# A two-layer decode step on one core: five load transfers merged at the two ends of its stream, and the last group's outgoing product made narrow

## The chip, the core and the metric

The kernel runs on one core of a Trainium2 chip. The metric is device time in microseconds, the median of the runs shown. Inside the core five engines work side by side: TensorE (PE in the profile, its weight loads PEld), VectorE (DVE), ScalarE (ACT), GpSimd (POOL) and SyncE (SP). All large loads are issued by SP and carried by 16 DMA engines into one big on-chip array, `arena`.

## The reference

One token goes through attention, MLP, attention, MLP. Both attention layers use the same weights and the same cache, and so do both MLPs. 32 heads, 4096 cached positions, head size 128, model width 512, MLP width 1376.

```
def _A_ref(x, k_cache, v_cache, wq, wo):
    q = (x @ wq).reshape(B, Sq, H, Dh)          # 1 token
    scores = einsum("bhqd,bhkd->bhqk", q, k_cache) * (Dh ** -0.5)
    o = einsum("bhqk,bhkd->bhqd", softmax(scores), v_cache)
    return o.reshape(B, Sq, H * Dh) @ wo
def _B_ref(x, w1, b1, w2, b2):
    return einsum("bsf,fd->bsd", gelu(x @ w1 + b1), w2) + b2
x = x + _A_ref(_layernorm(x), ...);  x = x + _B_ref(_layernorm(x), ...)
x = x + _A_ref(_layernorm(x), ...);  x = x + _B_ref(_layernorm(x), ...)
```

K and V are 64 MiB each. They don't fit on the chip, so almost all of both is read twice, in 32-bit floats.

## The kernel before, in words

The 32 heads are 8 groups of 4. A group's K is 8 blocks (`C = 8`) of 128 x 2048, 1 MiB each, and so is its V. Three regions of `arena` (A_AT, B_AT, C_AT) hold K and V in turn, so that SP can issue a load as soon as the region's former contents have been read. `load` (line 106) issues one transfer on SP; `blocks` (line 351) cuts a K or V into pieces and yields its blocks, and whoever uses a block waits for the whole piece that it came in.

For each group `group` (line 399) multiplies the queries with the 8 K blocks (`scores`: four 8 x 512 products per block), takes the softmax (`exponentials`, `weights`: a chain of small steps on DVE, one activation on ACT, four transposes on PE), and `values` multiplies the weights with V blocks (four 4 x 512 products per block). In most groups PE does two or three V blocks and DVE the others (`weighted`, `added`), and their sum and the outgoing product with wo of group n ride inside the scores of group n+1: behind block 4 comes `sum_up` with `head`, and `out_product` comes behind block 6, in the last group behind block 7.

The last group of each layer is different: PE does all 8 V blocks, V comes in the pieces of `LAST` (line 54), K in two halves, and two dummy products `idle(pS)` (128 x 512, no result) stand behind V blocks 5 and 7. Then comes `head_out` with a narrow outgoing product (16 products of 1 x 128 instead of 4 of 128 x 512), and the MLP (`mlp`): four w1 steps, the gelu on DVE and ACT, and 11 w2 blocks of four 1 x 128 products each, followed by the sum and the store of the result.

At the change of layers the loads share little room: `load_w1(SHARED, 3, 4)` may be issued only when `head` has read its scratch (line 290), the pieces of w2 (`W2_AT_CHANGE`) only when a w1 step has been read, and the next layer's weights and K (`behind_w2`) behind w2 blocks 3, 7 and 9. At the end, w1 and w2 (`W1_AT_END`, `W2_AT_END`, lines 53 and 56) go to free room and are issued early.

Each engine runs its instructions in the order in which the code emits them where `keep_in_program_order` is used: all loads on SP, all products on PE. What a block waits for is set by which piece it is in; what SP waits for is set by region reuse and by a ring of eight completion semaphores, each of which must be free before it is used again.

Small values live in two tiles, `cells` and `front`; `small` (line 83) puts them in the gaps of `cells`. The maximum `m` of the softmax lies in such a gap, inside the 128 columns that the wide outgoing product reads as its weights, so that in the last group line 233 waits for that product.

Of the kernel before, what the change touches and what calls it, by code (L numbers as in the profile page):

```python
# [23 lines left out]
C = 8  # L24
# [21 lines left out]
HALVES = ((0, 4), (4, 8))  # L46
# [4 lines left out]
FRONT = 192  # L51
CELLS = 239
W1_AT_END = ((0, 2), (2, 3), (3, 4))
LAST = ((0, 4), (4, 6), (6, 7), (7, 8))
W2_AT_CHANGE = ((0, 2), (2, 5), (5, 8), (8, 10), (10, 11))
W2_AT_END = ((0, 4), (4, 8), (8, 10), (10, 11))


@with_exitstack
def decode_layers(ctx: ExitStack, tc: tile.TileContext, vectors, k, v, w, w1, w2, out):  # L60
# [13 lines left out]
    ident, zq, wide = front[:, :P], front[:, P : P + ZQ], cells[:, :WIDE]  # L74
# [8 lines left out]
    def small(name, n=1):  # L83
        nonlocal first_front, rest
        if name.startswith("gelu_"):
            i = "huaztg".index(name[-1])
            return cells[:, gelu + FB * i : gelu + FB * (i + 1)]
        if name not in places:
            fit = [j for j in range(J) if gaps[j] + n <= ends[j]]
            if name == "by_dma":  # L90
                places[name] = front, first_front, n
                first_front += n
            elif fit:
                places[name] = cells, gaps[fit[0]], n
                gaps[fit[0]] += n
            else:
                places[name] = cells, rest, n
                rest += n
        t, a, m = places[name]
        assert m == n and first_front <= FRONT and rest <= CELLS  # L100
        return t[:, a : a + n]

    def at(first, n):
        return arena[:, first : first + n]

    def load(first, src):
        t = at(first, src.shape[-1])
        tc.keep_in_program_order(nc.sync.dma_start(t, src))  # L108
        return t

    def matmul(*a, **kw):
        tc.keep_in_program_order(nc.tensor.matmul(*a, **kw))  # L112
# [4 lines left out]
    def part(src, g, a, b):  # L117
        return src[g][:, NC * a : NC * b]
# [11 lines left out]
    by_dma = small("by_dma", FB + 8)  # L130
# [13 lines left out]
    pS, pO = (psum.tile([P, 512], F32, name=n) for n in ("pS", "pO"))  # L144
# [10 lines left out]
    def of_32(t, n, i=0):  # L155
        return t[:, : 32 * n].rearrange("p (c q) -> p c q", q=32)[:, :, i]

    def in_quarters(t, n):
        return t[:, : 32 * J].rearrange("p (j n) -> p j n", j=J)[:, :, :n]
# [4 lines left out]
    def turned(src, wide=False, to=None):  # L164

        t = turned_at[0] if to is None else to
        if wide:
            for j in range(J):
                q = slice(32 * j, 32 * j + 32)
                turn = nc.vector.transpose(t[q], src[q, P * j : P * (j + 1)])  # L170
                if src is pS:
                    tc.keep_in_program_order(turn)
        else:
            nc.vector.transpose(t, src[:, :P])  # L174
        return t
# [108 lines left out]
    def head(rl, last=False):  # L284
        ot = at(SCRATCH, U)
        nc.vector.transpose(ot, pO)  # L286
        o, on = small("o", 4), on_wide
        own = at(SCRATCH, 4 * 129).rearrange("p (b q) -> p b q", q=129)[:, :, :P]
        own = own.rearrange("p b (d q) -> p d b q", q=32)[:, :, :, 0]
        nc.vector.tensor_reduce(o, own, axis=AX.X, op=ALU.add)  # L290
        if last:
            nc.vector.tensor_scalar(on[:, :4], o, rl, None, op0=ALU.mult)  # L292
        else:
            nc.vector.tensor_scalar(in_quarters(on, 4), o.unsqueeze(1).to_broadcast([P, J, 4]), rl, None,
                                    op0=ALU.mult)
        return on
# [7 lines left out]
    def out_product(on, wt, to, narrow=False):  # L304
        for d in range(4):
            if narrow:
                for j in range(J):
                    matmul(to[32 * j : 32 * j + 1, :P], on[:, d : d + 1], wt[:, d, P * j : P * (j + 1)],
                           start=(d == 0), stop=(d == 3))
            else:  # L310
                matmul(to, on[:, d : d + P], wt[:, d, :], start=(d == 0), stop=(d == 3))
# [47 lines left out]
    def blocks(src, g, home, pieces=((0, C),)):  # L359
        for a, b in pieces:  # L360
            load(home + NC * a, part(src, g, a, b))
            for c in range(a, b):
                yield c, quarters(home + NC * c)
# [29 lines left out]
    def add_up(acc, own):  # L393
        t = small("acc", 4)
        nc.vector.scalar_tensor_tensor(t, own, 1.0, acc, op0=ALU.mult, op1=ALU.add)
        return t


    def group(z, acc, ahead, k_blocks, out_behind=C - 2):
        for c, t in k_blocks:  # L400
            scores(z, c, t)
            if ahead and c == SUM_BEHIND:
                t, rl, wt = ahead
                sum_up(t)
                on = head(rl)
            if ahead and c == out_behind:
                out_product(on, wt, pO)
        p = exponentials(sc, nsc)
        if ahead:
            acc = add_up(acc, of_32(turned(pO, wide=True), 4))  # L410
        return acc, *weights(p)

    def partly(pt, v_blocks, home, by_pe=BY_PE):
# [6 lines left out]
    negm, z, sc, nsc = first_queries(xs, s, wq_t, wide=True)  # L420
    acc = pairs(xs)[:, :, 0]
    ahead = None
    for g in range(G):
        final = g == G - 1
        k_home, v_home = RING[2 * g % 3], RING[(2 * g + 1) % 3]
        acc, pt, rl = group(z, acc, ahead, blocks(k, g, k_home, HALVES if final else ((0, C),)))
        ahead = None
        if g == G - 2:
            nc.scalar.copy(at(KEPT_K, 2 * U), at(k_home + NC * C - 2 * U, 2 * U))
        if g < G - 2:  # L430
            partly(pt, blocks(v, g, v_home), v_home)
            pair = load(PAIR, of_w(g % 2, g, 2))
            z = next_queries(xs, negm, by_four(pair[:, NC:]), to=pS)
            ahead = added(v_home), rl, by_four(pair[:, :NC])
            continue
        for c, t in blocks(v, g, v_home, LAST if final else ((0, C),)):
            values(c, pt, t, c)
            if final and c in (5, 7):
                idle(pS)
            if g == G - 2:  # L440
                for j in range(J):
                    i = 4 * c + j - KEPT_V // U
                    if i >= 0:
                        nc.scalar.copy(pK[i], t[j])
        if final:
            wo_t = by_four(load(PAIR, of_w(g % 2, g, 1)))
            for i in range(3):
                load_w1(SHARED, i, i + 1)
            own = head_out(rl, wo_t, last=True, home=ident)
            load_w1(SHARED, 3, 4)  # L450
        else:
            pair = load(PAIR, of_w(g % 2, g, 2))
            acc = add_up(acc, head_out(rl, by_four(pair[:, :NC])))
            wq_t = by_four(pair[:, NC:])
            z = next_queries(xs, negm, wq_t)
# [25 lines left out]
    g = G - 2  # L481
    negm, z, sc, nsc = first_queries(xs, s, wq_t)
    make_identity(nc, ident)
    acc = pairs(xs)[:, :, 0]
# [14 lines left out]
    pt, rl = weights(p)  # L499
# [3 lines left out]
    acc = add_up(acc, of_32(turned(pO), 4))  # L503

    v_t = [at(B_AT + U * i, U) for i in range(KEPT_V // U)]
    for i, first in enumerate([SHARED, SHARED + U] + [PAIR + U * j for j in range(4)]):
        t = at(first, U)
# [4 lines left out]
    pt, rl = weights(exponentials(sc, nsc))  # L512
    for c in range(C):
        values(c, pt, v_t[4 * c : 4 * c + 4], c)
    acc = add_up(acc, head_out(rl, by_four(pair[:, NC:])))
    z = next_queries(xs, negm, by_four(pair[:, :NC]))

    turned_at[0] = at(TURNED, P)
    homes, ahead = (A_AT, C_AT, B_AT), None
    for n in range(2, G):  # L520
        g, final = G - 1 - n, n == G - 1
        k_home, v_home = homes[(2 * n - 1) % 3], homes[2 * n % 3]
        acc, pt, rl = group(z, acc, ahead, blocks(k, g, k_home, HALVES if final else ((0, C),)),
                            C - 1 if final else C - 2)
        if not final:
            by_pe = BY_PE_AT_BEGIN if n == 2 else BY_PE
            partly(pt, blocks(v, g, v_home, ((0, 6), (6, 8)) if n == 2 else ((0, C),)), v_home, by_pe)
            pair = load(PAIR, of_w(g % 2, g - 1, 2))
            z = next_queries(xs, negm, by_four(pair[:, :NC]), to=pS)
            ahead = added(v_home, by_pe), rl, by_four(pair[:, NC:])  # L530
            continue
        for c, t in blocks(v, g, v_home, LAST):
            values(c, pt, t, c)
            if c in (5, 7):
                idle(pS)
        wo_t = by_four(load(PAIR, of_w(g % 2, g, 1)))
        for a, b in W1_AT_END:
            load_w1(A_AT, a, b)
        for a, b in W2_AT_END:
            load_w2(A_AT + 11 * U, a, b)  # L540
        own = head_out(rl, wo_t, last=True)
# [46 lines left out]
```

## Time and profile before

| | us |
|---|---|
| device time, three runs | 673.83, 673.91, 1145.31 |
| median | 673.91 |
| profiled execution, first to last instruction (its span) | 670.3 |
| DMA queue of SP, share of 16 engines | 99.1% |
| PE busy | 384.4 |
| DVE busy | 372.6 |
| loaded from memory | 285.6 MB |

Of the profiled execution the page gives the span and not the time around it; the two undisturbed runs are 3.5 and 3.6 us above the span. One run of 1145.31 lies far from the others; the median is not moved by it.

In the rows, a line number is that of the kernel printed above; all products issued through the helper have line 112 and all loads line 108, so they are told apart by their shapes. A row of a timeline gives start, duration, engine, line, operation, output and input, the count of merged instructions, and in brackets the idle time before it and what ended it. One product of the code is two matrix instructions in the trace. PEclk is the granted TensorE clock, 1.00 for full speed. Shares of DMA in short stretches can pass 1.00, since a packet's bytes and time are spread over it.

### The profile page before, as it was taken

What the parts mean: (1) busy time and instruction counts of PE and PEld (TensorE: products, weight loads), DVE (VectorE), ACT (ScalarE), POOL (GpSimd) and SP (SyncE); (2) the same over time, 40 slices, a digit from 0 to 9 for tenths busy, and PEclk for the clock granted to TensorE, in tenths of its full rate; (3) what the DMA queues carried; (4) which work ended last, traced back from release to release, by engine and by line L of the source; (5) the groups of instructions that cost most, each with busy time, mean ns of one, the idle gap of its engine ahead of it and who ended that gap; (6) DMA issues with size and microseconds to landing.
All of it is one profiled execution on the core that took longest, in us unless ns stands there. A gap on an engine that the chain in (4) does not pass through costs nothing. (4 is left out here: it accounts for less than half of the span.)

```text
span 670.3 us, 5537 instructions
## 1 busy us (share of the span) xinstructions
PE 384.4 (57%) x2342; PEld 109.2 (16%) x2342; DVE 372.6 (56%) x480; ACT 22.8 (3%) x48; POOL 4.8 (1%) x23
## 2 busy tenths in 40 slices
PE   3533842636618546286768878737617456074586
PEld 1101210101102101021214222111102112011122
DVE  2059388395793965932112221392893966938822
ACT  0010000000000000002000110000000000000000
POOL 1000000000000000000000000000000000000000
PEclk9567785877678658778979998977669868687789
DMA  9999999999999999999999999999999999999996
GB/s 376 438 439 438 434 438 438 405 464 435 438 430 408 430 438 439 438 438 421 426 416 402 431 452 423 437 440 431 426 434 416 457 439 438 435 423 407 438 420 286
DMA packets 11256, 285.97 MB, mean 427 GB/s; under 512 B 1504, under 2 KB 1504, under 8 KB 3296
## 3 DMA queue, kind: packets, MB, share of 16 engines
q1 hardware_dynamic: 11088, 285.61, 99.1%
q8 instruction: 18, 0.29, 0.2%
q14 instruction: 6, 0.05, 0.0%
q10 hardware_dynamic: 144, 0.01, 0.0%
HBM read 285.62 MB, written 0.00 MB: 426 GB/s over the span
## 5 line engine op out<-in xcount | busy, mean ns | idle before, releaser
L264 DVE TENSOR_TENSOR arena<-arena 128x2048 f32<-128x2048 f32 (+4 forms) x44 | 260.7, 5924 | 16.6 <-DMA arena<-in_v 15.9
L112 PE MATMUL pS<-arena,front 128*8 128x512 f32 x1036 | 152.0, 713 | 174.9 <-DMA arena<-in_k 164.5
L112 PE MATMUL pO<-arena 128*4 128x512 f32 x504 | 81.7, 800 | 26.1 <-DMA arena<-in_v 24.5
L112 PE MATMUL pO<-arena,cells 128*128 128x512 f32 (+4 forms) x376 | 82.7, 506 | 17.2 <-POOL cells L186 6.7
L112 PEld LDWEIGHTS pS<-arena,front 128*8 128x8 f32 x1036 | 30.6, 102 | 289.1 <-DVE arena L264 141.9
L286 DVE STREAM_TRANSPOSE arena<-pO 128x512 f32<-128x512 f32 x16 | 11.5, 717 | 110.1 <-PE pO L112 110.1
L112 PE MATMUL pS<-arena,cells 128*1 128x128 f32 (+1 forms) x328 | 55.8, 385 | 18.5 <-DMA arena<-in_w 15.8
L170 DVE STREAM_TRANSPOSE arena<-pO 32x128 f32<-32x128 f32 x64 | 20.0, 312 | 59.0 <-PE pO L112 58.4
L112 PEld LDWEIGHTS pO<-arena,cells 128*128 128x128 f32 (+3 forms) x376 | 28.7, 122 | 64.7 <-issue 35.8
L230 DVE TENSOR_REDUCE cells<-pS 128x1 f32<-128x512 f32 x16 | 11.1, 692 | 50.1 <-PE pS L112 49.8
L244 PE MATMUL pO<-front,arena 128*128 128x128 f32 x64 | 12.0, 318 | 46.2 <-ACT arena L239 46.2
L112 PEld LDWEIGHTS pS<-arena,cells 128*1 128x1 f32 (+1 forms) x328 | 23.9, 120 | 61.2 <-issue 52.8
L239 ACT ACTIVATE arena<-pS,cells 128x512 f32<-128x512 f32 x16 | 12.4, 777 | 507.1 <-DVE cells L235 507.1
L112 PEld LDWEIGHTS pO<-arena 128*4 128x4 f32 x504 | 13.5, 99 | 76.2 <-issue 66.3
L244 PEld LDWEIGHTS pO<-front,arena 128*128 128x128 f32 x64 | 7.6, 154 | 60.2 <-ACT arena L239 59.1
L170 DVE STREAM_TRANSPOSE arena<-pS 32x128 f32<-32x128 f32 x44 | 13.7, 312 | 1.6
L249 DVE STREAM_TRANSPOSE cells<-cells 128x32 f32<-128x32 f32 x16 | 3.4, 214 | 15.9 <-ACT arena L239 15.7
L390 DVE MEMSET pS<- 128x512 f32 x11 | 5.3, 485 | 1.2
L174 DVE STREAM_TRANSPOSE arena<-pS 128x128 f32<-128x128 f32 x3 | 1.0, 317 | 8.9 <-PE pS L112 8.9
L199 DVE TENSOR_SCALAR cells<-cells,pS 128x4 f32<-128x4 f32 x4 | 0.9, 234 | 7.9 <-PE pS L112 7.9
L112 PE MATMUL pO<-arena,front 128*128 128x128 f32 (+2 forms) x18 | 5.1, 382 | 0.0
L247 DVE COPY arena<-pO 128x128 f32<-128x128 f32 x16 | 4.2, 261 | 0.7 <-PE pO L244 0.5
(62 smaller groups left out, 72.5 us busy)
## 6 DMA issues: line engine op xcount, KB each, us to landing
arena<-in_w SPq DMA_DIRECT2D x13, 2048.0 KB, 11.2
arena<-in_k SPq DMA_DIRECT2D x4, 4096.0 KB, 24.9
arena<-in_v SPq DMA_DIRECT2D x2, 4096.0 KB, 38.7
arena<-in_w SPq DMA_DIRECT2D x6, 1024.0 KB, 21.1
arena<-in_v SPq DMA_DIRECT2D x3, 2048.0 KB, 42.5
arena<-in_v SPq DMA_DIRECT2D x1, 6144.0 KB, 30.2
arena<-in_w SPq DMA_DIRECT2D x6, 688.0 KB, 25.9
arena<-in_v SPq DMA_DIRECT2D x4, 1024.0 KB, 46.0
```

The lines of the kernel that those rows point to most:

```text
L112: tc.keep_in_program_order(nc.tensor.matmul(*a, **kw))
L170: turn = nc.vector.transpose(t[q], src[q, P * j : P * (j + 1)])
L174: nc.vector.transpose(t, src[:, :P])
L199: nc.vector.tensor_scalar(xc, pairs(xs)[:, :, 0], nm, None, op0=ALU.add)
L230: nc.vector.tensor_reduce(ml[:, 0:1], pS, axis=AX.X, op=ALU.max)
L239: nc.scalar.activation(p, pS, AF.Exp, bias=bias[:, 0:1], scale=sc, accum_out=ml[:, 0:1])
L244: tc.keep_in_program_order(nc.tensor.transpose(pT[:, b].rearrange("p j r -> p (j r)"), p[:, P * b : P * (b + 1)], ident))
L247: nc.vector.tensor_copy(pt, pT[:, :, :, :C].rearrange("p b j c -> p c j b"))
L249: nc.vector.transpose(lt, ml)
L264: tc.keep_in_program_order(nc.vector.tensor_tensor(*a, **kw))
L286: nc.vector.transpose(ot, pO)
L390: nc.vector.memset(pS, 0.0)
```

## The change

- K of the second layer's last group comes in one transfer of 8 MiB instead of two of 4.
- V of that group comes in two halves instead of pieces of 4, 2, 1 and 1 blocks. Its two dummy products stand behind blocks 3 and 7.
- w2 at the end comes in pieces of 8, 2 and 1 blocks instead of 4, 4, 2 and 1.
- V of the first layer's last group comes in pieces of 5, 2 and 1 blocks instead of 4, 2, 1 and 1; its dummy products stand behind blocks 4 and 7. K there stays in halves.
- The outgoing product that rides in the second layer's last group (that of the group before it) is narrow: 16 products of 1 x 128, no copies of the head's output, and one transpose instead of four.
- `m` moves from `cells` to `front`, in all groups.

```diff
-LAST = ((0, 4), (4, 6), (6, 7), (7, 8))
+LAST, LAST_AT_END = ((0, 5), (5, 7), (7, 8)), ((0, 4), (4, 8))
-W2_AT_END = ((0, 4), (4, 8), (8, 10), (10, 11))
+W2_AT_END = ((0, 8), (8, 10), (10, 11))
...
-            if name == "by_dma":
+            if name in ("by_dma", "m"):
...
-    def group(z, acc, ahead, k_blocks, out_behind=C - 2):
+    def group(z, acc, ahead, k_blocks, final=False):
         for c, t in k_blocks:
             scores(z, c, t)
             if ahead and c == SUM_BEHIND:
                 t, rl, wt = ahead
                 sum_up(t)
-                on = head(rl)
-            if ahead and c == out_behind:
-                out_product(on, wt, pO)
+                on = head(rl, last=final)
+            if ahead and c == C - 1 - (not final):
+                out_product(on, wt, pO, narrow=final)
         p = exponentials(sc, nsc)
         if ahead:
-            acc = add_up(acc, of_32(turned(pO, wide=True), 4))
+            acc = add_up(acc, of_32(turned(pO, wide=not final), 4))
...
             values(c, pt, t, c)
-            if final and c in (5, 7):
+            if final and c in (4, 7):
                 idle(pS)
...
-        acc, pt, rl = group(z, acc, ahead, blocks(k, g, k_home, HALVES if final else ((0, C),)),
-                            C - 1 if final else C - 2)
+        acc, pt, rl = group(z, acc, ahead, blocks(k, g, k_home), final)
...
-        for c, t in blocks(v, g, v_home, LAST):
+        for c, t in blocks(v, g, v_home, LAST_AT_END):
             values(c, pt, t, c)
-            if c in (5, 7):
+            if c in (3, 7):
                 idle(pS)
```

On PE, in the first layer's last group (the 8 x 512 rows are its scores, L244 the transposes of the softmax weights, the 4 x 512 rows its V blocks at four each, the 128 x 512 rows the dummy products):

```order
 L112 MATMUL pS<-arena,front 8x512 x32
 L244 MATMUL pO<-front,arena 128x128 x4
-L112 MATMUL pO<-arena 4x512 x24
+L112 MATMUL pO<-arena 4x512 x20
 L112 MATMUL pS<-arena,front 128x512
-L112 MATMUL pO<-arena 4x512 x8
+L112 MATMUL pO<-arena 4x512 x12
 L112 MATMUL pS<-arena,front 128x512
```

The first dummy product now stands behind five V blocks instead of six.

On PE, in the second layer's last group, from the sum of the group before (the 4 x 512 row on `cells`) to the second dummy product:

```order
 L112 MATMUL pO<-arena,cells 4x512 x4
 L112 MATMUL pS<-arena,front 8x512 x12
-L112 MATMUL pO<-arena,cells 128x512 x4
+L112 MATMUL pO<-arena,cells 1x128 x16
 L244 MATMUL pO<-front,arena 128x128 x4
-L112 MATMUL pO<-arena 4x512 x24
+L112 MATMUL pO<-arena 4x512 x16
 L112 MATMUL pS<-arena,front 128x512
-L112 MATMUL pO<-arena 4x512 x8
+L112 MATMUL pO<-arena 4x512 x16
 L112 MATMUL pS<-arena,front 128x512
```

The outgoing product keeps its place behind the last scores and changes its shape; the first dummy product stands two V blocks earlier.

On SP, the last loads of the program (in_k and in_v are K and V of the last group, the three in_w rows of 2048, 2752 and 1376 are wo and w1, those behind them w2):

```order
 L108 DMA arena<-in_w 128x4096
-L108 DMA arena<-in_k 128x8192 x2
-L108 DMA arena<-in_v 128x8192
-L108 DMA arena<-in_v 128x4096
-L108 DMA arena<-in_v 128x2048 x2
+L108 DMA arena<-in_k 128x16384
+L108 DMA arena<-in_v 128x8192 x2
 L108 DMA arena<-in_w 128x2048
 L108 DMA arena<-in_w 128x2752
 L108 DMA arena<-in_w 128x1376 x2
-L108 DMA arena<-in_w 128x2048 x2
+L108 DMA arena<-in_w 128x4096
```

The bytes and their order stay; four issues are gone here, and one more in the first layer's V.

## The prediction

> **What bounds the kernel now.** I read the page's head first, then the chain of waits from its end, then the stretches of the DMA and of the clock, then the timelines of the two places that the change touches. The page:
>
> ```profile
> span 670.3 us, 5537 instructions
> DMA  9999999999999999999999999999999999999996
> q1 hardware_dynamic: 11088, 285.61, 99.1%
> ```
>
> The DMA engines work through the whole span: 285.61 MB set the time. A change saves time where it gives the stream fewer microseconds, and costs time where it makes the stream pause or lengthens what comes behind its last byte. The view of stretches (PE, PEld, DVE, ACT, POOL busy, PEclk, DMA share, GB/s) shows the stream with whole K and V, with halves, and at the change of layers:
>
> ```profile
> 570.00:600.00 30.00, 14.02 (x84) 3.60 (x82) 20.28 (x15) 0.00 (x0) 0.00 (x0) 0.72 0.99 427
> 612.00:640.00 28.00, 16.38 (x82) 3.65 (x81) 22.37 (x15) 0.00 (x0) 0.00 (x0) 0.76 0.99 425
> ...
> 360.00:370.00 10.00, 8.20 (x144) 4.40 (x140) 3.13 (x17) 0.21 (x1) 0.72 (x4) 1.00 1.00 393
> ```
>
> Whole and half pieces run at 427 and 425; at the change of layers the rate falls to 393, so there the stream is already thin. The list of issues (KB each, us from issue to landing) says the same:
>
> ```profile
> arena<-in_k SPq DMA_DIRECT2D x4, 4096.0 KB, 24.9
> ...
> arena<-in_w SPq DMA_DIRECT2D x2, 768.0 KB, 5.8
> ...
> out<-cells SPq DMA_DIRECT2D x1, 2.0 KB, 1.4
> ```
>
> Most loads stand in the queue for tens of microseconds; the w2 pieces at the change of layers (768 KB) land 5.8 us after their issue, of which their own bytes take 1.8 (at 427) and a bare transfer 1.4 (the store of 2 KB). The queue's lead there is about 2.6 us at most. The end, in the chain of waits:
>
> ```profile
> 647.61 18.66 DMA arena<-in_w
> 666.27 0.04 issue
> 666.32 0.62 PE pS L112 x16
> 666.93 0.04 issue
> 666.97 0.44 PE pS L112 x8
> ```
>
> w2 blocks 8 and 9 land at 666.27, block 10 at 666.93, and PE has caught up with both.
>
> **The clock.** A third of the argument hangs on PEclk, so I cut the end into stretches of 3.4 us:
>
> ```profile
> 631.50:634.90 3.40, 2.35 (x16) 0.42 (x16) 1.40 (x1) 0.00 (x0) 0.00 (x0) 0.50 0.98 424
> 634.90:638.30 3.40, 3.40 (x20) 0.61 (x16) 1.13 (x3) 0.00 (x0) 0.00 (x0) 0.50 0.86 371
> 638.30:641.70 3.40, 3.40 (x14) 1.25 (x7) 0.91 (x2) 0.00 (x0) 0.00 (x0) 1.00 1.05 448
> ...
> 344.70:348.10 3.40, 3.40 (x33) 0.68 (x25) 0.00 (x0) 0.00 (x0) 0.00 (x0) 0.99 0.99 419
> ...
> 641.70:645.10 3.40, 1.27 (x4) 0.34 (x3) 1.99 (x9) 0.87 (x2) 0.10 (x1) 1.00 0.96 407
> 645.10:648.50 3.40, 3.02 (x16) 0.85 (x19) 0.96 (x6) 0.00 (x0) 0.00 (x0) 0.50 1.01 426
> ...
> 662.20:665.60 3.40, 2.24 (x54) 1.25 (x57) 1.43 (x6) 0.21 (x1) 0.00 (x0) 1.00 0.82 331
> ```
>
> It is 0.50 or 1.00 and changes on this grid. PE busy 1.27 of 3.40 at full clock is followed by half clock; 2.35 at half clock isn't enough to get out of it, 3.02 and 3.40 are; 2.24 at full clock keeps it. A run of products after a wait is thus slow until one whole window has been nearly full, and a wait that leaves a window under some 1.4 us of work shuts the clock for the next. What a block costs, and the first layer's last group:
>
> ```profile
> 327.65 7.05 PE L112 MATMUL pS<-arena,front 128*8 128x512 f32 x64 [1.65 <-DVE front L220]
> ...
> 340.82 7.25 PE L112 MATMUL pO<-arena 128*4 128x512 f32 x48 [2.66 <-DMA arena<-in_v]
> 348.00 1.12 PE L112 MATMUL pS<-arena,front 128*128 128x512 f32 x2
> ...
> 350.46 1.04 PE L112 MATMUL pO<-arena 128*4 128x512 f32 x8 [0.36 <-DMA arena<-in_v]
> ...
> 359.58 0.76 PE L112 MATMUL pO<-arena,cells 128*2 128x344 f32 x8 [0.27 <-DMA arena<-in_w]
> ```
>
> ```profile
> 351.57 0.72 DVE L286 STREAM_TRANSPOSE arena<-pO 128x512 f32<-128x512 f32 x1 [13.01 <-PE pO L112]
> ...
> 352.56 0.33 SPq L108 DMA_DIRECT2D arena<-in_w  x1
> ```
>
> Eight blocks in 7.05 us are 0.87 each at full clock, so 1.74 at half.
>
> **Part by part.** *Fewer transfers.* The five merges cost the stream at most the difference of 427 and 425, 0.5% of 19.6 us (8.39 MB), 0.09 us each time a K or V is whole instead of cut; w2 and the first V less. I take 0.2 us for all five, between 0 and 0.4. The Trainium skill ("DMA: Bandwidth & Descriptors", "Anatomy of one DMA") gives a transfer about 2 us of fixed cost; by that five would save 10 us if nothing overlapped, which the DMA shares of 0.99 in both rows speak against.
>
> *V of the first layer in 5, 2 and 1.* Before, PE starts on block 0 at 340.82 when four blocks are there, and the clock opens at 344.7; it is done with six blocks at 348.1 and then follows the stream: it waits 0.36 us for block 7, and DVE's line 286 starts at 351.57. With five blocks in the first piece it starts 2.43 us later (from 340.7 to 350.4 four blocks came), at 343.2. The window to 344.7 is then only 1.5 us busy and the clock stays half until 348.1: 2.8 blocks by then, 2.2 more at 0.87 to 350.0, the dummy product (1.05) to 351.05, blocks 5 to 7 at 0.87 to 353.65, line 286 at 353.9: 2.3 us late. With the windows elsewhere it is 1.3 to 2.5. Who waits: `load_w1(SHARED, 3, 4)` (line 450), issued at 352.56 when line 290 is through, and behind it on SP every load of the change of layers: the w2 pieces, the next weights, the next K. PE gives back the 0.3 us that it waits for w1 at 359.58, and some 0.4 before the narrow product. 1.6 us remain at this phase. What of them reaches the stream: nothing, if the queue's lead of up to 2.6 us covers it; all, if the lead is used up, as the 393 GB/s say that it is. That row is the nearest, since it is the sum over all engines where the lead is the slowest one's. I take 1.6, and 0.8 to 2.0 over the phases. Behind it the stream is full again and gives nothing back, so it goes to the end.
>
> *K whole, narrow product, V in halves.* These lie on the path of PE:
>
> ```profile
> 630.70 1.20 PE L112 MATMUL pS<-arena,front 128*8 128x512 f32 x8 [3.88 <-DMA arena<-in_k]
> ...
> 639.12 3.70 PE L112 MATMUL pO<-arena,cells 128*128 128x512 f32 x8
> 644.95 1.00 PE L244 MATMUL pO<-front,arena 128*128 128x128 f32 x4 [2.13 <-ACT arena L239]
> ...
> 656.93 1.05 PE L112 MATMUL pS<-arena,cells 128*1 128x128 f32 x32 [0.26 <-DVE cells L292]
> ...
> 661.95 1.12 PE L112 MATMUL pS<-arena,front 128*128 128x512 f32 x2
> 664.24 1.93 PE L112 MATMUL pS<-arena,cells 128*1 128x128 f32 x64 [1.16 <-DVE cells L339]
> ```
>
> ```profile
> 642.86 0.16 DVE L233 TENSOR_REDUCE cells<-cells 128x1 f32<-128x8 f32 x1 [2.65 <-PE pO L112]
> ```
>
> K whole puts four more blocks behind its landing (630.66): 2.4 blocks at half clock to 634.9, 5.6 at 0.87 and the sum's 0.9 to 640.7, 1.6 later than now. The narrow product takes 1.05 (656.93) instead of 3.70, and with `m` in `front` line 233 doesn't wait for it: 2.65 less, and 0.3 for the transpose that now stands before line 235. The softmax's transposes come at 643.8 instead of 644.95: 1.1 us early. V's second half lands with the last block now, when PE is just there (four blocks and a dummy product, 651). All of that is hidden under the stream, which ends when it ends; if K whole cost its four blocks at half clock (7.0) and the product saved nothing, PE would be 5 us late and 4 would show.
>
> *w2's first eight blocks in one.* Now blocks 0 to 3 are there early and PE runs eight blocks from 664.24 on. Merged, nothing can start before blocks 4 to 7 land, 1.2 us (0.52 MB) ahead of 666.27, at 665.05, less 0.2: 664.9. From there 11 blocks at 0.24 (1.93 for eight) are 2.65, the end of PE at 667.55 against 667.41: 0.1 us more at full clock. But PE's dummy product ends 1 us earlier than its 663.07, so it idles from some 662.2 to 664.9, 2.7 us. A window that holds this gap has at most 0.7 us of work, less than the 1.27 that shut the clock at 645.1. If the clock shuts in mid-run, 5 to 8 of the blocks take 0.24 more: 1.4 to 1.9 in all; if just ahead of it, all eleven: 2.7. If the gap lies across a window's edge it stays open: 0.1. Stepping the edge through 3.4 us gives 3 in 10 for open, 6 for mid-run, 1 for the whole run. The Trainium skill ("TensorE: Matmul & The Clock Gate", "Part 1: The HAM clock gate") has the clock go back to half only after an idle window of about 3.4 us; by that it would stay open here and the tail cost 0.1. The trace disagrees: 1.27 us of work did not keep it open.
>
> *Sum*, against the span of 670.3: both losses hang on one grid, and a late stream moves the second place against it. With this trace's phase the first place costs 1.6 and moves the gap to 663.8 to 666.5, across the edge at 665.6: tail 0.1, in all 1.7. Where the first is cheap (0.8 to 1.2) the second is mostly dear (1.4 to 1.8). Stepped through, the sum has its middle at 2.2, half of it between 1.3 and 2.6. I take 2.1: 672.4 in the span, and with the 3.6 us between it and the median, 676.0.
>
> **Rivals.** *The stream has cover at the change of layers* and the clock stays open at the end: +0.1, 674.0. For it the 2.6 us of lead; against it 393 GB/s. *Faster*: the stream saves 0.4, the lead covers the first place, and the tail costs 0.1 at full clock: 673.6. What decides is whether PE reaches line 286 by 351.6 plus the lead; against it, five blocks at half clock. Saving 2 us a transfer (664) belongs here, with almost no chance. *Slower*: both places meet their bad phase, the gap shuts the clock ahead of w2's run and the change of layers costs 2: +4.7, 678.6. For it the 1.27 row, against it that one phase in ten does it. *Nothing but the tail*: +1.6, 675.5, from cover at the first place alone; it lies inside the forecast.
>
> **How the numbers follow.** Forecast (675.0 to 677.6) 0.62, cover 0.16, faster 0.10, slower 0.12. The range takes in the forecast and the case of cover: 673.9 to 677.9. Within 2%, 13.5 us, lie all of them; a difference of about 2% is what a measurement of this kernel can tell from none. I leave 0.01 for faster and 0.02 for slower beyond it, for what is not seen here.
>
> **What would show it.** Line 286 of the first layer's last group at 353 to 354 and the next SP issue a microsecond behind it; a lower rate than 393 at 360 to 370; PEclk 0.50 up to 348. In the last group, line 233 right behind line 232, and in w2's run one wait for in_w followed by eleven blocks, with PEclk below 1.00 in it or not. I am wrong if line 286 is late and the rate of the stream behind it does not fall, or if PE starts w2's run later than its landing.

## The result, and the profile after

The changed kernel takes 676.75 us (median of 6 runs, 675.24 to 678.66), the kernel before 673.4 beside it; the ratio is 1.0061, 95% interval 1.0045 to 1.0077, so 4.1 us slower, 3.0 to 5.2. A few executions that took far longer (1145.31 and 697.71 of the kernel before, 762.4 and 837.22 in two experiments) are left out of all ratios. In every run of the changed kernel the time is 1.73 to 1.78 us above that execution's span. The profiled one took 676.96.

The page after:

```profile
span 675.2 us, 5571 instructions
q1 hardware_dynamic: 10368, 285.61, 98.5%
```

The bytes are the same, the span is 4.9 us longer, and SP's queue is busy 98.5% of it instead of 99.1%. 0.6% of 675 is 4 us: it is all time in which the stream stood still or had ended.

**The change of layers.** TensorE's timeline of the changed kernel, from the first layer's last V to the w2 pieces (start, duration, operation, idle time before and what ended it):

```profile
343.30 6.27 PE L112 MATMUL pO<-arena 128*4 128x512 f32 x40 [3.95 <-DMA arena<-in_v]
349.50 1.12 PE L112 MATMUL pS<-arena,front 128*128 128x512 f32 x2
350.56 2.76 PE L112 MATMUL pO<-arena 128*4 128x512 f32 x24
...
361.29 1.12 PE L112 MATMUL pS<-arena,front 128*128 128x512 f32 x2
...
364.97 0.84 PE L112 MATMUL pS<-arena,cells 128*1 128x128 f32 x24 [0.82 <-DMA arena<-in_w]
...
366.89 0.84 PE L112 MATMUL pS<-arena,cells 128*1 128x128 f32 x24 [0.46 <-DMA arena<-in_w]
```

Stretches of the same kernel (the fields as in the prediction; the eighth, behind the five busy times, is PEclk):

```profile
340.10:347.00 6.90, 3.70 (x20) 0.75 (x24) 0.00 (x0) 0.00 (x0) 0.00 (x0) 0.51 0.91 388
347.00:350.00 3.00, 3.00 (x25) 0.69 (x18) 0.00 (x0) 0.00 (x0) 0.00 (x0) 1.00 1.00 421
360.00:370.00 10.00, 7.58 (x122) 3.75 (x122) 2.02 (x9) 0.21 (x1) 0.22 (x2) 1.00 0.95 342
```

The five blocks wait for their piece until 343.30, run at half clock to 347.0, and the rest follows without a wait. VectorE reads the product late, in the row of line 286:

```profile
353.38 0.72 DVE L286 STREAM_TRANSPOSE arena<-pO 128x512 f32<-128x512 f32 x1 [13.59 <-PE pO L112]
```

That was 351.57 before: 1.8 us late. The rate of the next stretch is 342 GB/s where it was 393. Now the issues on SP behind it, first before, then after (start, time on SP, transfer, how many in a row):

```profile
352.56 11.39 SPq L108 DMA_DIRECT2D arena<-in_w  x7
365.52 9.17 SPq L108 DMA_DIRECT2D arena<-in_k  x6
376.94 0.33 SPq L108 DMA_DIRECT2D arena<-in_w  x1
387.97 0.33 SPq L108 DMA_DIRECT2D arena<-in_k  x1
```

```profile
354.38 11.60 SPq L108 DMA_DIRECT2D arena<-in_w  x7
367.79 9.15 SPq L108 DMA_DIRECT2D arena<-in_k  x6
379.18 0.33 SPq L108 DMA_DIRECT2D arena<-in_w  x1
390.22 0.33 SPq L108 DMA_DIRECT2D arena<-in_k  x1
```

The first issue is 1.82 late, the first one of K 2.27, and the next two rows 2.24 and 2.25: the stream gives nothing of it back. TensorE does, for a while. The row at 361.29, the dummy product behind w1, stands 1.02 us later than before; the two rows of the kernel before that belong beside the rows at 361.29 and 366.89 are:

```profile
360.27 1.12 PE L112 MATMUL pS<-arena,front 128*128 128x512 f32 x2
...
364.62 0.84 PE L112 MATMUL pS<-arena,cells 128*1 128x128 f32 x24 [0.21 <-DMA arena<-in_w]
```

Behind it TensorE waits 0.82 and 0.46 us for two pieces of w2, which SP had issued 1.46 and 1.36 us late (358.53 and 360.09 instead of 357.07 and 358.73), and the product at 366.89 is 2.27 late. The first issue of K stands 0.06 us behind that product's end, in both kernels.

**The end.** TensorE's timeline of the changed kernel's last group, with VectorE's two rows of the maximum behind it:

```profile
634.03 5.98 PE L112 MATMUL pS<-arena,front 128*8 128x512 f32 x40 [15.65 <-DMA arena<-in_k]
...
643.26 1.05 PE L112 MATMUL pO<-arena,cells 128*1 128x128 f32 x32
...
654.09 3.62 PE L112 MATMUL pO<-arena 128*4 128x512 f32 x32 [0.42 <-DMA arena<-in_v]
...
664.04 1.12 PE L112 MATMUL pS<-arena,front 128*128 128x512 f32 x2
668.06 4.11 PE L112 MATMUL pS<-arena,cells 128*1 128x128 f32 x88 [2.89 <-DMA arena<-in_w]
```

```profile
644.24 0.21 DVE L232 STREAM_TRANSPOSE cells<-cells 128x32 f32<-128x32 f32 x1
644.49 0.16 DVE L233 TENSOR_REDUCE front<-cells 128x1 f32<-128x8 f32 x1
```

The narrow product takes 1.05 us, and line 233 stands right behind line 232 without the 2.65 us wait. TensorE has caught up with V at 654.09, and 2.89 us of idle time stand ahead of w2's run. The chain of waits of the same kernel ends there:

```profile
641.73 26.19 DMA arena<-in_w
667.92 0.14 issue
668.06 4.16 PE pS L112 x88
```

All eleven blocks now lie behind one landing, and they take 4.16 us. Its stretches:

```profile
664.40:667.80 3.40, 0.77 (x2) 0.00 (x0) 1.31 (x6) 0.21 (x1) 0.00 (x0) 1.00 0.78 316
667.80:671.20 3.40, 3.14 (x60) 2.18 (x64) 0.00 (x0) 0.00 (x0) 0.00 (x0) 0.50 0.07 29
671.20:675.00 3.80, 0.96 (x36) 0.58 (x24) 0.48 (x2) 0.00 (x0) 0.00 (x0) 0.95 0.02 1
```

The window with the gap holds 0.77 us of work, the next runs at half clock under 60 of the 88 matrix instructions, and after that full one the clock is whole again.

### The profile page after: what moved, and what is told of

The parts are those of the page before. It is cut to its first block, busy times and chain, and to the rows that moved or that the text cites. A ratio compares the mean times of both kernels' runs of the same rounds, so it can differ in the third digit from the quotient of the medians.

```text
span 675.2 us, 5571 instructions
## 1 busy us (share of the span) xinstructions
PE 386.9 (57%) x2366; PEld 111.5 (17%) x2366; DVE 371.3 (55%) x477; ACT 22.8 (3%) x48; POOL 4.8 (1%) x23
## 3 DMA queue, kind: packets, MB, share of 16 engines
q1 hardware_dynamic: 10368, 285.61, 98.5%
## 5 line engine op out<-in xcount | busy, mean ns | idle before, releaser
L112 PE MATMUL pS<-arena,front 128*8 128x512 f32 x1036 | 147.9, 696 | 172.8 <-DMA arena<-in_k 169.1
L112 PE MATMUL pO<-arena 128*4 128x512 f32 x504 | 84.4, 824 | 30.2 <-DMA arena<-in_v 28.6
L112 PE MATMUL pO<-arena,cells 128*128 128x512 f32 (+4 forms) x400 | 81.0, 481 | 16.2 <-POOL cells L186 7.1
L112 PE MATMUL pS<-arena,cells 128*1 128x128 f32 (+1 forms) x328 | 62.4, 428 | 20.1 <-DMA arena<-in_w 18.4
L112 PEld LDWEIGHTS pO<-arena,cells 128*2 128x2 f32 (+3 forms) x400 | 28.6, 118 | 61.9 <-issue 34.9
L112 PEld LDWEIGHTS pS<-arena,cells 128*1 128x1 f32 (+1 forms) x328 | 26.6, 134 | 67.3 <-issue 59.6
L244 PE MATMUL pO<-front,arena 128*128 128x128 f32 x64 | 11.1, 298 | 45.9 <-ACT arena L239 45.9
L244 PEld LDWEIGHTS pO<-front,arena 128*128 128x128 f32 x64 | 7.0, 145 | 59.5 <-ACT arena L239 58.3
```

Of the source, the lines that this page charges most:

```text
L244: tc.keep_in_program_order(nc.tensor.transpose(pT[:, b].rearrange("p j r -> p (j r)"), p[:, P * b : P * (b + 1)], ident))
```

## The experiments

The theory: the change loses time at two places that have nothing to do with each other, the change of layers (the first V in a piece of five makes TensorE late for the product that lets SP issue on) and the end (w2's merged piece leaves a gap that shuts the clock). The rivals: one of them carries it all; the merged transfers cost by themselves; the last group's K, V and narrow product are not hidden. The first four runs take the edits apart.

**The first V back.** The changed kernel with:

```
-LAST, LAST_AT_END = ((0, 5), (5, 7), (7, 8)), ((0, 4), (4, 8))
+LAST, LAST_AT_END = ((0, 4), (4, 6), (6, 7), (7, 8)), ((0, 4), (4, 8))
-            if final and c in (4, 7):
+            if final and c in (5, 7):
```

> The changed kernel, with only the first layer's last V back in pieces of 4, 2, 1 and 1 and its first dummy product back behind block 5. Theory (both places cost: a slow clock makes PE late at the change of layers, where the queue has no lead, and the clock shuts ahead of w2's run at the end): line 286 of the first layer's last group back at about 351.6 from 353.4, the next load of SP back at about 352.6 from 354.4, the weights behind w2 at the change of layers about 2 us earlier, and 2 us less in the span than the changed kernel, 1.5 more than before. Rival (all of the loss sits at the end): no less than 0.5 us gained. Rival (larger pieces cost by landing later, not by the clock): nothing gained either, since the last piece lands at the same time.

Measured: 674.67, ratio 1.0027 (1.0017 to 1.0038). Line 286 is back at 351.57 and the first K issue at 365.74; what is left, 1.8 us, is the end. Its w2 run in TensorE's timeline, and the stretches around it:

```profile
665.76 4.87 PE L112 MATMUL pS<-arena,cells 128*1 128x128 f32 x88 [3.53 <-DMA arena<-in_w]
```

```profile
660.90:664.30 3.40, 1.32 (x6) 0.30 (x2) 1.53 (x6) 0.21 (x1) 0.00 (x0) 1.00 0.93 386
664.30:667.70 3.40, 1.94 (x40) 1.37 (x44) 0.00 (x0) 0.00 (x0) 0.00 (x0) 0.50 0.30 121
667.70:671.10 3.40, 2.93 (x56) 1.69 (x48) 0.37 (x2) 0.00 (x0) 0.00 (x0) 0.50 0.00 0
```

Here 1.32 us of work shut the clock ahead of the run, and since the run began in the middle of a window, neither window was full and it stayed at half to the end: 4.87.

**w2's pieces back.** The changed kernel with:

```
-W2_AT_END = ((0, 8), (8, 10), (10, 11))
+W2_AT_END = ((0, 4), (4, 8), (8, 10), (10, 11))
```

> The changed kernel, with only w2 at the end back in pieces of 4, 4, 2 and 1. Theory: PE starts w2's run on the first four blocks about 2.4 us ahead of the landing of the next four, so the wait ahead of it falls from 2.9 us to about 1 and the clock stays at 1.00; from the landing of blocks 8 and 9 to the end of PE about 1.2 us, and 1.5 to 2 us less than the changed kernel, 2 more than before. Rival (the loss sits at the change of layers alone): 0.1 us gained. Rival (the narrow product or K whole makes PE late): PE would start w2's run later than 666.3 and nothing is gained.

Measured: 675.26, 1.0039 (1.0026 to 1.0052): 2.6 us remain for the change of layers, where line 286 comes at 352.85 and the first K issue at 366.95. The two single losses, 1.8 and 2.6, make 4.4, and both together were 4.1: they add up within the intervals. In the profiled execution the clock shut under the last blocks here too. TensorE's rows of w2, and the stretch that they begin in:

```profile
664.58 1.05 PE L112 MATMUL pS<-arena,cells 128*1 128x128 f32 x32 [1.30 <-DMA arena<-in_w]
666.79 3.04 PE L112 MATMUL pS<-arena,cells 128*1 128x128 f32 x56 [1.15 <-DMA arena<-in_w]
```

```profile
663.60:667.00 3.40, 1.27 (x40) 0.97 (x44) 0.41 (x3) 0.21 (x1) 0.00 (x0) 1.00 0.80 326
667.00:670.00 3.00, 2.83 (x56) 1.85 (x45) 0.12 (x1) 0.00 (x0) 0.00 (x0) 0.50 0.03 13
```

With pieces of four it still waited 1.30 and 1.15 us, and 1.27 us of work were left in the window: pieces of four do not protect the clock in every execution either, and the 2.6 us are not the change of layers alone.

**Both back.** Left of the change are K whole, V in halves, the narrow product and `m` in `front`.

> The changed kernel with the first V and w2 both back as before; what is left is K whole, V in halves, the narrow product and m in front, in the last group of the second layer. Theory: all of it is hidden under the stream of loads, so within 0.5 us of the kernel before, rather below it; line 233 follows line 232 without a wait and PE is about 1 us early in the last group. Rival (K whole costs its four blocks at half clock on the path that sets the end): 1 to 4 us slower than before.

Measured: 672.84, 1.0000 (0.9991 to 1.0009). These four edits together cost or save no more than 0.6 us. The rival that they are not hidden falls.

**The first V alone.** The kernel before with:

```
-        for c, t in blocks(v, g, v_home, LAST if final else ((0, C),)):
+        for c, t in blocks(v, g, v_home, LAST_FIRST if final else ((0, C),)):
```

where `LAST_FIRST` is 5, 2 and 1 blocks and the first layer's dummy stands behind block 4.

> The kernel before with only the first layer's last V in pieces of 5, 2 and 1 and its first dummy product behind block 4. Theory: 1 to 2 us slower than before, with line 286 1.3 to 2.5 us late and the stream's rate at the change of layers lower by as much. Rival (the queue's lead covers it): no difference in the span, though line 286 is late.

Measured: 675.94, 1.0040 (1.0025 to 1.0055), 2.7 us. This edit alone is more than I had forecast for it, though line 286 (one line lower in this file) is only 1.15 us late, at 352.72. In the profiled execution the late stream also met the end badly. Its last seven w2 blocks in TensorE's timeline:

```profile
667.72 3.17 PE L113 MATMUL pS<-arena,cells 128*1 128x128 f32 x56 [1.74 <-DMA arena<-in_w]
```

They take 3.17 us for the 56 instructions that at full clock take 1.6 (0.24 a block), so part of the 2.7 us is the end's.

**The clock at the end, pieces unchanged.** The changed kernel with two dummy products more ahead of the last w2 run:

```
-        idle(pS)
+        for _ in range(1 if load_w2 else 3):
+            idle(pS)
```

> The changed kernel with two more dummy products (128 x 512, no result) on PE behind the one that stands ahead of w2's run at the end; all else as in the changed kernel, w2's first eight blocks still in one. Theory (the clock shuts in the wait for w2): the products fill about 2.1 of the 2.9 us of wait, PEclk stays at 1.00, the eleven blocks take 2.6 us instead of 4.2, and 1.3 to 1.7 us are gained against the changed kernel. Rival (the loss there is the later landing of the merged piece): nothing gained, the run starts and ends as before.

Measured: 675.85, 1.0045 (1.0028 to 1.0062). The run in TensorE's timeline, and its stretches:

```profile
667.30 2.58 PE L112 MATMUL pS<-arena,cells 128*1 128x128 f32 x88 [1.63 <-DMA arena<-in_w]
```

```profile
663.60:667.00 3.40, 2.07 (x5) 0.57 (x3) 0.94 (x5) 0.21 (x1) 0.00 (x0) 1.00 0.81 329
667.00:670.40 3.40, 2.58 (x88) 2.23 (x88) 0.41 (x2) 0.00 (x0) 0.00 (x0) 1.00 0.07 28
```

The same 88 instructions behind the same merged piece take 2.58 instead of 4.11, with no more in front of them than useless work. That the half clock of the run was the gap's, and not the merged transfer's, is shown. The median against the changed kernel's gained less than these 1.5 us, and the two kernels' intervals overlap. By the ratio 3.0 us are left, of which the lateness of line 286 in the profiled execution, 1.4 us at 352.99, explains about half. That execution was the fastest of the four (674.66, the others 675.78 to 675.99), so what the others lost is not known.

**The clock at the change of layers, pieces unchanged.** The changed kernel with two dummy products ahead of the first layer's last V:

```
+        for _ in range(2 if final else 0):
+            idle(pS)
```

> The changed kernel with two dummy products on PE between the softmax and the V blocks of the first layer's last group, where PE waits 4 us for the piece of five blocks. Theory (the clock is what makes PE late): PEclk is at 1.00 one window (3.4 us) earlier, line 286 comes 1 to 2 us earlier than in the changed kernel although the piece lands no earlier, and 1 to 2 us are gained. Rival (the later landing of five blocks makes PE late): line 286 as late as in the changed kernel or later by the dummy products, nothing gained.

Measured: 674.75, 1.0036 (1.0023 to 1.0048). TensorE's row of the five blocks, and the two stretches ahead of it and under it:

```profile
343.15 4.47 PE L112 MATMUL pO<-arena 128*4 128x512 f32 x40 [1.75 <-DMA arena<-in_v]
```

```profile
337.70:341.10 3.40, 3.40 (x7) 1.23 (x5) 0.75 (x5) 0.00 (x0) 0.00 (x0) 0.50 1.17 506
341.10:344.50 3.40, 1.65 (x17) 0.42 (x20) 0.00 (x0) 0.00 (x0) 0.00 (x0) 0.99 0.84 361
```

With a full window ahead, the piece of five lands at the same time and its blocks take 4.47 instead of 6.27; line 286 comes at 351.44 and the first K issue at 365.27, both earlier than in the kernel before. So the piece of five makes TensorE late only through the clock. What is left is the end, which this kernel still has (4.25 us for w2's run). Its ten times fall into two groups, six from 673.94 to 674.77 and four from 676.1 to 676.83; only one execution was profiled, so that the clock's window lay badly in the second group is argued, not shown.

**Both dummies.**

> The changed kernel with the dummy products of both places. Theory: both gains, about 3 us less than the changed kernel, within 1 us of the kernel before, with all five transfers still merged. Rival (the merges themselves cost): as slow as the changed kernel.

Measured: 673.25, 1.0009 (1.0000 to 1.0019). The end ran at full clock (2.58), but in the profiled execution the front did not:

```profile
339.30:342.70 3.40, 2.35 (x3) 0.34 (x1) 0.00 (x0) 0.00 (x0) 0.00 (x0) 0.50 1.03 443
342.70:346.10 3.40, 2.86 (x16) 0.60 (x20) 0.00 (x0) 0.00 (x0) 0.00 (x0) 0.50 0.96 410
```

The same two dummies that filled a window before lay across an edge here, 2.35 us of 3.40, and line 286 came at 352.93. The windows do not lie at the same place in each execution.

**w2's pieces alone.** The kernel before with w2 in 8, 2 and 1 blocks.

> The kernel before with only w2's first eight blocks in one transfer. Theory: the wait ahead of w2's run grows from 1.2 us to about 1.9, since PE is not early here; a window around it still has 1.5 us of work, so the clock mostly stays open and the cost is 0.1 to 0.4 us in most runs, up to 2 where the window's edge falls badly. Rival (the merged piece costs as much by itself): 1.5 to 2 us slower whatever the wait.

Measured: 672.76, 1.0012 (0.9998 to 1.0027). Its w2 run in TensorE's timeline, and the stretch in which it begins:

```profile
665.17 2.58 PE L112 MATMUL pS<-arena,cells 128*1 128x128 f32 x88 [3.30 <-DMA arena<-in_w]
```

```profile
663.30:666.70 3.40, 1.53 (x57) 1.50 (x61) 0.00 (x0) 0.00 (x0) 0.00 (x0) 1.00 0.41 165
```

A wait of 3.30 us, longer than the changed kernel's, and the clock stays whole, since the gap lay across an edge and neither window fell below 1.5 us of work. Six of its ten runs are within 0.35 us of 672.5, three from 674.31 to 675.99.

**TensorE late, nothing merged.** Is it TensorE's lateness that makes the pause, or the piece of five as a transfer? The kernel before, pieces unchanged, with three dummies instead of one behind V block 5 of the first layer:

```
-                idle(pS)
+                for _ in range(3 if c == 5 else 1):
+                    idle(pS)
```

> The kernel before, its pieces of values unchanged (4, 2, 1 and 1 blocks in the first layer's last group), with three dummy products instead of one behind block 5, so that TensorE comes later to the layer's outgoing product though no transfer is merged. The two dummies take about 1.1 us each at full clock, of which the wait for the next piece hides a part. Theory (the pause at the change of layers is nothing but TensorE's lateness, since the second layer's first weights wait for the first layer's last division): line 286 about 1.5 to 2 us later than in the kernel before, the issue of the second layer's weights as much later, the rate from 360 to 370 us lower, and the time 1.5 to 2.5 us above the kernel before, ratio about 1.003. Rival (it is the piece of five blocks as a transfer that costs, by how it spreads the engines of the queue): the time within 0.5 us of the kernel before, although line 286 is late.

Measured: 674.3, 1.0013 (1.0001 to 1.0025): 0.9 us by the ratio, between the 1.5 to 2.5 that I expected and the rival's 0.5. The profile fell on the execution of 837 us and isn't read, so line 286 isn't known. I doubled the step, to five dummies:

> The kernel before, its pieces unchanged, with five dummy products instead of one behind block 5 of the first layer's last V: the same step as in the run with three, twice as large. Four more dummies at 1.1 us, less the 0.4 us for which TensorE waits there now and what else the wait hid, put line 286 about 3.7 us later (355.3 instead of 351.6). Theory (each microsecond of TensorE's lateness there is one of pause in the stream, beyond a lead that the queue keeps, which by the run with three dummies, 0.9 to 1.4 us slower for about 1.6 us late, is 0.2 to 0.7 us): 3.0 to 3.5 us above the kernel before, ratio about 1.0048. Rival (lateness without a merged transfer costs little, and the loss at this place comes with the piece of five): 1 us or less above the kernel before.

Measured: 676.91, 1.0064 (1.0050 to 1.0078), 4.3 us, more than the 3.0 to 3.5 that I expected. Its rows of line 286, of SP's issues, and of the stretch from 360 to 370:

```profile
354.96 0.72 DVE L286 STREAM_TRANSPOSE arena<-pO 128x512 f32<-128x512 f32 x1 [15.82 <-PE pO L112]
```

```profile
355.96 11.31 SPq L108 DMA_DIRECT2D arena<-in_w  x7
369.31 9.23 SPq L108 DMA_DIRECT2D arena<-in_k  x6
```

```profile
360.00:370.00 10.00, 7.67 (x108) 3.90 (x108) 1.75 (x8) 0.21 (x1) 0.55 (x1) 1.00 0.89 320
```

3.4 us of lateness at line 286, 3.8 at the first K issue, 4.3 in the time, with all of the old pieces: lateness alone makes the pause. The rival of the piece as such falls.

**Four transfers fewer without either loss.** The first V as before, the rest of the change, and the two dummies ahead of w2's run.

> The changed kernel with the first layer's last V back in 4, 2, 1 and 1 blocks, and two more dummy products ahead of the run over w2: four transfers fewer than before, without the late outgoing product at the change of layers and without the half clock under the last eleven blocks. Theory (the loss is two late places, and nothing else): the run over w2's last blocks takes 2.6 us, and the time is that of the kernel before within 0.4 us either way, ratio 0.9994 to 1.0006. Rival (a merged piece costs by itself, since the work behind it is one lump that starts later): 0.5 to 1.5 us above the kernel before, with the run at full clock. Third: the saved transfers now show, 0.2 us or more below.

Measured: 672.68 beside 672.9, ratio 0.9995 (0.9986 to 1.0003). At 2.58 us for w2's run nothing of the loss shows in the time; the four merges together cost no more than 0.2 us and save no more than 0.9.

**Three dummies ahead of the first V.** As with both dummies, but three in front.

> The changed kernel with all pieces merged, two more dummies ahead of w2's run, and three dummies (instead of the two of an earlier run) ahead of the first layer's last V, so that the window of the clock in front of the piece of five is busy enough wherever it begins. Theory (what was left in the run with two was executions in which the window fell so that the clock stayed at half): line 286 near 351.5 us, the clock whole from about 341 us, and a time within 0.5 us of the kernel before, below that of the run with two. Rival (the rest is the lump of five itself, not the clock): the clock whole and still 0.5 to 1 us above the kernel before.

Measured: 673.06, 1.0001 (0.9991 to 1.0010), all ten runs from 672.37 to 673.59. The five blocks take 4.47 us again, and line 286 comes at 351.58. With the clock held at both places the whole change, five merges and all, takes the time of the kernel before.

**All profiled executions together.** The first K issue of the second layer carries the first place, and what lies from there to the span's end carries the second. In the order of that difference; the last column counts from the landing of w2's last piece (the last of its 16 engines in the trace's landing records) to the span's end:

| kernel | line 286 | first K issue | span | span less K issue | clock under w2's last run | last landing to end |
|---|---|---|---|---|---|---|
| before | 351.57 | 365.52 | 670.3 | 304.8 | whole | 3.4 |
| w2's pieces alone | 351.52 | 365.72 | 670.8 | 305.1 | whole | 3.9 |
| both dummies | 352.93 | 367.08 | 672.4 | 305.3 | whole | 3.9 |
| four fewer | 351.77 | 365.91 | 671.3 | 305.4 | whole | 4.0 |
| three dummies | 351.58 | 365.79 | 671.2 | 305.4 | whole | 3.9 |
| dummies at the end | 352.99 | 367.12 | 672.9 | 305.8 | whole | 3.9 |
| five dummies, TensorE late | 354.96 | 369.31 | 675.1 | 305.8 | whole | 3.4 |
| both back | 351.47 | 365.80 | 671.7 | 305.9 | whole | 3.6 |
| w2's pieces back | 352.85 | 366.95 | 672.9 | 305.9 | half, for 7 blocks | 4.3 |
| dummies in front | 351.44 | 365.27 | 672.3 | 307.0 | half | 5.6 |
| first V alone | 352.72 | 366.89 | 673.9 | 307.0 | half, for 7 blocks | 4.4 |
| the change | 353.38 | 367.79 | 675.2 | 307.4 | half | 5.4 |
| first V back | 351.57 | 365.74 | 673.7 | 308.0 | half | 6.2 |

With the clock whole, 304.8 to 305.9 us follow the first K issue, whatever its time; with half clock 305.9 to 308.0. The change's excess is 2.27 us of K's issue and, from the mean of the whole-clock rows (305.4) to 307.4, 2.0 us of the end: 4.3, beside 4.1 measured in the times. The kernel before has the lowest of these sums, which makes the difference of the two profiles, 4.9, somewhat larger than the true one.

The last column parts the cases without overlap: 3.4 to 3.6 us with the clock whole and w2 in pieces of four, 3.9 to 4.0 whole with the merged piece, 4.3 and 4.4 with half clock under seven blocks, 5.4 to 6.2 with half clock under the merged run. So of the 2.0 us that the change loses at the end, some 0.5 is the later start of the merged run and 1.5 the clock.

## Why the prediction was right or wrong

The time, 676.0 forecast and 676.75 measured, lies in the range. The difference that was forecast does not fit so well: 2.1 us against 4.1. The time came out near because of a second error that went the other way. I put 3.6 us between the span of 670.3 and the median, taken from two different executions; what lies around a span is 1.75, so the profiled execution of the kernel before was itself one of about 672.05. With 1.75 the forecast would have been 674.15, at the low edge of the range: that 676.0 came within 0.8 us of the measured time is luck. The intervals of the ratios here reach 0.1 to 0.2% either way, so the prediction's 2%, as the least difference that a measurement of this kernel can tell, is far too wide.

Step by step:

- *The stream bounds the kernel, the queue's lead at the change of layers is used up*: right. Each K issue stays late by what SP was late, and the rate from 360 to 370 fell from 393 to 342 GB/s. The rival with cover is refuted by the five dummies without a merged transfer.
- *The piece of five starts at 343.2, at half clock*: right, 343.30, and shown by the dummies in front. The clock opened at 347.0 instead of 348.1, so line 286 was 1.8 us late instead of 2.3 (whose steps, added up, end at 353.7 and give 2.2); in the four other executions with this piece and a late clock it was 1.2 to 1.4.
- *"PE gives back the 0.3 us that it waits for w1 at 359.58, and some 0.4 before the narrow product. 1.6 us remain"*: this step failed. TensorE did give back 0.8 us: it was 1.02 late at 361.29. But this does not reach the stream. SP had by then issued w2's pieces 1.46 and 1.36 late, TensorE waits for them (0.82 and 0.46 at 364.97 and 366.89), and the first K issue, which stands behind the second, is 2.27 late. In the run with five dummies line 286 is 3.4 late and K 3.8. Over all the profiled executions K's issue is as late as line 286: seven have line 286 on time, between 351.44 and 351.77, and K at 365.68 in the mean (365.27 to 365.91); against these means four with line 286 1.2 to 1.4 late have K late by the same within 0.05, the change has 2.1 for 1.8 and the five dummies 3.6 for 3.4. Whether the lateness also grows on the way can't be told from differences that small. Nor is it known why the second piece was used 6.8 us after its issue, and 5.9 before, though the DMA engines were less busy (0.95 from 360 to 370, 1.00 before). The size of the term was 2.1 to 2.3, not 1.6.
- *K whole, V in halves, the narrow product, hidden*: right, ratio 1.0000 with these alone.
- *Fewer transfers, 0.2 us*: not contradicted; four fewer gave 0.9995 (0.9986 to 1.0003). The Trainium skill ("DMA: Bandwidth & Descriptors", "Anatomy of one DMA") gives about 2 us of fixed cost for a transfer that GpSimd issues; here SP issues them. At that price four would have saved 8 us, so in this full queue no such cost was there to be saved.
- *w2's first eight blocks in one*: the mechanism was right and the choice among its prices wrong. I saw the gap of 2.7 us (it was 2.89 and ran from about 665.2), the window that would shut, and 1.4 to 1.9 us for a clock shut in the run; then I took "With this trace's phase the first place costs 1.6 and moves the gap to 663.8 to 666.5, across the edge at 665.6: tail 0.1". The windows' edges are not a property of the kernel: they were at 662.2 and 665.6 in the profile before and at 664.4 and 667.8 in that after, and the two runs with the same two dummies in front fell on different sides of one. The tail cost 2.0 by the table. With the clock whole the merged piece costs some 0.5 and not 0.1, and the 2.7 that I priced for a clock shut just ahead of the run was too high: that is what happened (shut at 667.8, run from 668.06), and the clock cost 1.5, 4.11 against 2.58, since one nearly full window opens the clock again. The dearest case seen, 4.87 with the first V back, cost 2.3; there the run began in the middle of a window.
- *The clock follows the window's work, not idleness alone*: right. Windows with 0.77, 1.27 and 1.32 us of 3.40 were followed by half clock, those with 1.53, 2.07 and 2.24 by whole. The border is not sharp in the trace's busy time: with the first V alone a window of 1.51 (663.3 to 666.7) was followed by half clock. The Trainium skill ("TensorE: Matmul & The Clock Gate", "Part 1: The HAM clock gate") asks for an idle window; by that the changed kernel's run would have stayed at full clock, and it did not.

So two terms were too small. Against the 1.7 of this trace's own phase, the change of layers cost 0.5 to 0.7 more (2.1 to 2.3 for 1.6) and the end 1.9 more (2.0 for 0.1); the 2.1 that I took, a middle over the phases, made up 0.4 of that. The two places were the forecast ones, and so was what goes wrong at each, but for what TensorE was to give back. The rival that prices both places badly, 4.7, came closest to what happened. I had given it 0.12, as a phase that one execution in ten meets; of the four profiled executions with w2 merged and nothing added ahead of it, three ran at half clock.

## What to carry to other kernels

A larger transfer costs where the engine behind it waits: the start moves to the landing of the last byte, and on TensorE the gap can halve the clock of what follows. Before merging pieces, find in the timeline which engine is waiting for the first of them, and what is issued only when that engine is through; in the full queue of this kernel four merges saved less than 1 us. Where loads are issued by the progress of an engine and that engine waits for those loads, count a late start in full, and don't price a clock's window by the edges of a single profile.

## What the runs showed of the hardware that was not expected

- The edges of the clock's windows lie differently in each execution, on one even grid: in the thirteen profiled executions other than that of 837 us, from 250 us on, a period of 3.413 us meets every change of PEclk. Of the whole windows at full clock, 801 were followed by full clock, with at least 1.42 us of TensorE work, and 212 by half, 210 of them with at most 1.38. At half clock 209 opened it, with at least 2.60 us, and 365 did not, with at most 2.83. So the work to keep it is some 1.4 us and that to open it some 2.6 to 2.8, about twice as long at half the clock.
- The ten times of one kernel, that with two dummies in front, fell into two groups about 2 us apart (673.94 to 674.77 and 676.1 to 676.83).
- A half clock under a short run needn't last: 60 of 88 instructions ran at half, and the rest at full, once one window had 3.14 of 3.40 us of work. A window with 1.94, where the run began in its middle, left the next at half.
- Useless products can pay for themselves: two dummies took w2's run from 4.11 to 2.58 us. They only restored what the merge had lost; no version here beats the kernel before by more than can be measured.
- In the trace's landing records the 16 DMA engines finish the last w2 piece up to 2.9 us apart before and 3.8 after; over the other profiled executions of usual length it was 2.7 to 4.2, without a clear relation to the pieces. Why it differs from one execution to the next is not settled.
